# A Strassen form of the first MLP product in the last four tiles of a transformer block, and a plan that keeps GpSimd and VectorE apart

## The chip, the cores and the metric

One core of one Trainium2 chip runs the whole block. The metric is the device time of one launch in microseconds. Before the change the median of three runs was 514.28 us (513.51 to 523.58).

## What is computed

A pre-norm transformer block in float32 on x of 2048 tokens by D = 512: h = x + A(LN(x)), out = h + MLP(LN(h)).

- A: qkv = LN(x) wqkv (512 x 1536); 32 heads of 16; each token attends to 8 keys, itself and every second token back (offsets 0, 2, ..., 14), masked below 0; softmax; then the product with wo (512 x 512).
- MLP: relu(LN(h) w1 + b1) squared, times w2, plus b2, with F = 1792.

Every matmul operand is split into a high part (float32r, a cast on ScalarE) and a low part (the operand minus its high part); a product is three passes, high x high, high x low and low x high.

## The kernel before, in words

The 2048 tokens are 16 tiles of 128 rows; four tiles make a group u (`R = 4`, `NU = 4`). The hidden axis is 14 blocks of 128 (`FB`), called f. For a group, `mlp1(f)` multiplies a block of w1 (stationary, four K-blocks of 128) by the transposed normalised rows of the group (moving, 512 columns, kept in `big` as four K-blocks): 12 matmuls of 512 columns. ScalarE then applies relu with the bias, squares, and casts to the high part `rh`; GpSimd (or VectorE in the last group) makes the low part `rl`. `mlp2(f)` multiplies each tile's 128 columns of `rh` and `rl` (stationary) by the block of w2 (moving, 512 columns) and adds into four PSUM banks `acc`: 12 matmuls of 512 columns again. It runs two blocks behind `mlp1` (`LAGW = 2`). Before the first group come the first products (qkv) and attention. Attention is done in items, one for a group of tiles and a quarter of the heads: VectorE multiplies and reduces 2048-element rows, GpSimd adds up the weighted values, the result goes through DRAM to be transposed (`turned`), then through the product with wo (`wo_product`, line 457 for all three-pass products), the second norm and a second transposition. `split_h` writes the high and low parts of the next group into `big` once the current group's `mlp1` is through with it. Sums of the first three groups are parked in DRAM (`park`, `park_h`) and brought together with h and b2 by `unpark` during the last group, two sums for each of 12 tiles.

PSUM has eight banks: six slots `ps` (four of them `acc` during an MLP), `qp` and `le`.

The order is not written out by hand. Each step is a task with the engines that may run it, an estimated time on each, the keys it reads and writes, and a due time: for TensorE's tasks their place in TensorE's sequence, for others the earliest due time behind them less durations, or a `by` that the caller gave, moved by a small random draw (`NOISE`, `SEED`). `schedule` then simulates the engines and puts, at each step, the task with the earliest start (then the earliest due time) on its engine; buffers of each tag are counted, and some are kept free for the most urgent task (`KEEP`, `SPARE`). Attention items are due at `need[u] - ITEM * (G - g) - BEFORE[u]`. The program is issued in the order of the simulated start times; every engine works its own queue in that order, and all loads and stores are issued from SP. The waits between engines follow from what the instructions read and write, in the order of issue. The last lines of the function finish the group tile by tile, the last tile in two halves of 256 columns (line 955).

## Time and profile before

| | before |
|---|---|
| median of the runs | 514.28 us |
| the profiled execution | 514.67 us |
| its span, first to last instruction | 512.9 us |
| TensorE busy | 501.9 us, 2300 matmuls |
| VectorE, ScalarE, GpSimd busy | 333.6, 292.0, 323.0 us |
| DMA | 127.7 MB, mean 249 GB/s |

The span is 1.8 us shorter than the execution's time; the rest lies around it. PE is TensorE's matmuls, PEld its weight loads, DVE VectorE, ACT ScalarE, POOL GpSimd. A line such as L327 or L332 is that of a helper (`lo`, `tt`), so groups are told apart by the names of their tiles.

### The profile page before, as it was taken

What the parts mean: (1) busy time and instruction counts of PE and PEld (TensorE: products, weight loads), DVE (VectorE), ACT (ScalarE), POOL (GpSimd) and SP (SyncE); (2) the same over time, 40 slices, a digit from 0 to 9 for tenths busy, and PEclk for the clock granted to TensorE, in tenths of its full rate; (3) what the DMA queues carried; (4) which work ended last, traced back from release to release, by engine and by line L of the source; (5) the groups of instructions that cost most, each with busy time, mean ns of one, the idle gap of its engine ahead of it and who ended that gap; (6) DMA issues with size and microseconds to landing.
All of it is one profiled execution on the core that took longest, in us unless ns stands there. A gap on an engine that the chain in (4) does not pass through costs nothing.

```text
span 512.9 us, 6775 instructions
## 1 busy us (share of the span) xinstructions
PE 501.9 (98%) x2300; PEld 419.2 (82%) x2300; DVE 333.6 (65%) x314; ACT 292.0 (57%) x552; POOL 323.0 (63%) x273
## 2 busy tenths in 40 slices
PE   8999999999998999999999999999999999999997
PEld 8998888888886888868888877888888887888885
DVE  6259898996979996988799979596022103446003
ACT  4538877759364654379843436974367645433341
POOL 6421659768697799899994789589755424223220
PEclk9999999999999999999999999999999999999999
DMA  7699698999979999768976486865462731999422
GB/s 243 179 277 297 148 301 274 348 356 402 335 290 334 326 363 353 224 224 300 324 258 220 168 289 237 272 217 184 129 203 86 251 116 41 305 358 408 160 81 82
DMA packets 82834, 127.73 MB, mean 249 GB/s; under 512 B 7280, under 2 KB 49776, under 8 KB 82800
## 3 DMA queue, kind: packets, MB, share of 16 engines
q1 hardware_dynamic: 82656, 127.17, 73.3%
q8 instruction: 18, 0.29, 0.2%
q14 instruction: 16, 0.13, 0.1%
q10 hardware_dynamic: 144, 0.13, 0.1%
HBM read 89.96 MB, written 37.36 MB: 248 GB/s over the span
## 4 chain that ended last, share of the span: by engine, by line
PE 72%; DMA 8%; ACT 6%; POOL 5%; DVE 4%; issue 3%; SPq 1%; POOLq 0%; ACTq 0%; DVEq 0%
PE mm L457 41%; PE acc L735 20%; PE wo L457 7%; POOL pr L621 3%; DMA k<-qkv_d 3%; DVE pr L572 2%; PE tr L401 2%; DMA back<-o_d 2%; PE tr L803 1%; DMA qkv_d<-y 1%; DMA xt<-in_A_x_dram 1%; DMA o_d<-o 1%; POOL rl L327 1%; ACT r L722 1%; ACT big_h L322 1%
## 5 line engine op out<-in xcount | busy, mean ns | idle before, releaser
L621 POOL TENSOR_TENSOR pr<-pr 128x1024 f32<-128x1024 f32 (+1 forms) x64 | 118.8, 1883 | 11.7 <-DVE pr L603 8.4
L327 POOL TENSOR_TENSOR rl<-r,rh 128x512 fp32r<-128x512 f32 x53 | 68.6, 1297 | 86.4 <-ACT rh L322 86.2
L735 PE MATMUL acc<-w2s,rh 128*128 128x512 f32 x444 | 110.7, 389 | 0.0
L722 ACT ACTIVATE r<-mm,b_sb 128x512 f32<-128x512 f32 x56 | 38.3, 687 | 120.8 <-PE mm L457 113.8
L735 PEld LDWEIGHTS acc<-w2s,rh 128*128 128x128 f32 x444 | 83.3, 188 | 17.3
L572 DVE TENSOR_TENSOR pr<-qp,k 128x2048 f32<-128x2048 f32 x32 | 72.7, 2275 | 18.2 <-POOL o L621 12.7
L577 DVE TENSOR_REDUCE le<-pr 128x128 f32<-128x2048 f32 x32 | 73.3, 2290 | 0.9
L603 DVE TENSOR_TENSOR pr<-le,v 128x2048 f32<-128x2048 f32 x32 | 72.1, 2279 | 1.7 <-POOL o L621 1.1
L735 PE MATMUL acc<-w2s,rl 128*128 128x512 f32 x222 | 60.4, 390 | 0.0
L457 PE MATMUL mm<-big_h,xl 128*128 128x512 f32 (+1 forms) x208 | 51.1, 376 | 0.0
L457 PE MATMUL mm<-big_h,xh 128*128 128x512 f32 (+1 forms) x208 | 50.5, 375 | 0.1
L457 PE MATMUL mm<-big_l,xh 128*128 128x512 f32 (+1 forms) x208 | 50.6, 375 | 0.0
L735 PEld LDWEIGHTS acc<-w2s,rl 128*128 128x128 f32 x222 | 41.7, 188 | 9.0 <-DVE rl L327 0.4
L457 PEld LDWEIGHTS mm<-big_h,xh 128*128 128x128 f32 x208 | 38.0, 188 | 6.6 <-ACT big_h L322 0.5
L457 PEld LDWEIGHTS mm<-big_l,xh 128*128 128x128 f32 x208 | 37.9, 188 | 5.3
L457 PEld LDWEIGHTS mm<-big_h,xl 128*128 128x128 f32 x208 | 37.8, 188 | 5.2
L428 DVE STREAM_TRANSPOSE turned<-back 128x512 f32<-128x512 f32 x26 | 17.8, 696 | 36.6 <-DMA back<-o_d 24.1
L322 ACT CAST rh<-r 128x512 fp32r<-128x512 f32 x56 | 34.6, 622 | 3.0 <-ACT r L724 0.4
L724 ACT ACTIVATE r<-r 128x512 f32<-128x512 f32 x56 | 35.2, 632 | 1.3
L457 PE MATMUL mm<-big_h 128*128 128x512 f32 x128 | 34.5, 391 | 0.3 <-ACT r L722 0.3
L457 PE MATMUL mm<-big_h,big_l 128*128 128x512 f32 x128 | 34.2, 389 | 0.0
L457 PE MATMUL mm<-big_l,big_h 128*128 128x512 f32 x128 | 34.2, 389 | 0.0
(104 smaller groups left out, 791.2 us busy)
## 6 DMA issues: line engine op xcount, KB each, us to landing
w2s<-w_d SPq DMA_DIRECT2D x56, 512.0 KB, 5.0
k<-qkv_d SPq DMA_DIRECT2D x16, 704.0 KB, 6.1
v<-qkv_d SPq DMA_DIRECT2D x16, 704.0 KB, 6.2
qkv_d<-y SPq DMA_DIRECT2D x18, 512.0 KB, 3.6
raw<-in_B_w_dram SPq DMA_DIRECT2D x28, 256.0 KB, 6.7
w_d<-w2s SPq DMA_DIRECT2D x14, 512.0 KB, 6.6
xt<-in_A_x_dram SPq DMA_DIRECT2D x16, 256.0 KB, 5.7
q<-qkv_d SPq DMA_DIRECT2D x16, 256.0 KB, 4.3
```

Source lines behind the costliest of these rows:

```text
L322: act(n, lambda: nc.scalar.copy(dst(), src()), r=r, w=w, **k)
L327: lambda e: engines[e].tensor_tensor(out=dst(), in0=src(), in1=h(), op=ALU.subtract), r=r, w=w, **k)
L401: nc.tensor.transpose(tr.get()[:, n, :], s(), ident)
L428: vec(D, lambda: nc.vector.transpose(dst.get(), src.get()[:, part]), r=[src], w=[dst, *w])
L457: nc.tensor.matmul(ps(), l(), rr(), start=start and i == 0, stop=stop and i == len(terms) - 1)
L572: vec(2048, lambda pr=pr, i0=i0: nc.vector.tensor_tensor(out=pr.get(), in0=qp.get()[:, i0:i0 + IQ].unsqueeze(2).to_broadcast([P, IQ, W, GC ...
L577: vec(2048, lambda pr=pr, i0=i0: nc.vector.tensor_reduce(out=lg()[:, i0:i0 + IQ].rearrange("p i w h -> p (i w h)"), in_=pr.get().rearrange ...
L603: vec(2048, lambda p2=p2, i0=i0: nc.vector.tensor_tensor(out=p2.get(), in1=window(vs.get(), i0, [DH, GH], [1, DH]), op=ALU.mult, in0=ex()[ ...
L621: nc.gpsimd.tensor_tensor(out=dst, in0=a, in1=b_, op=ALU.add)
L722: act(D, lambda: nc.scalar.activation(r.get(), ps.get(), AF.Relu, bias=b1_sb[:, f:f + 1]), 0.08, r=[ps, "b1"], w=[r], keep=2)
L724: act(D, lambda: nc.scalar.activation(r.get(), r.get(), AF.Square), w=[r])
L735: nc.tensor.matmul(acc[j].get(), l.get()[:, j * P:(j + 1) * P], w2s.get()[:, wn], start=lead and n < len(js), stop=end and n >= len(terms) ...
```

## The change

In the last group the fourteen blocks f are taken in seven pairs (`WIN`). A pair's first product, a 256 x 512 by 512 x 512 product, is computed by the Winograd form of Strassen's scheme: both operands are cut into 2 x 2 blocks of 256 x 256, and seven products of sums stand for eight of blocks. A block product is 6 matmuls of 256 columns (two K-blocks, three passes), accumulated in half a PSUM bank. The sums of w1's blocks are made for each pair from raw weights that are loaded again (`win_weights`), one operand of each sum lying in PSUM, and their high and low parts go where wo's were. The sums of the rows are made once, on GpSimd or VectorE (`win_rows`), into two of the three `pr` buffers. The seven products are combined by seven sums on VectorE and one copy on ScalarE (`win_pair`), then follow relu, square and the split as before. The two sums of a parked tile move from VectorE to GpSimd. The plan no longer lets GpSimd and a VectorE task that is marked `port` (two operands in SBUF) overlap in its simulation, and hands a GpSimd task to VectorE when that ends sooner. The random draws come from one seed for each 40 us, and several constants of the plan are others.

```diff
-ITEM = 18.0
-BEFORE = 8, 4, 12, 8
+ITEM = 16.0
+BEFORE = 8, 16, 4, 16
 X_BY_DRAM = (14, 15)
-W2_EACH = 6.0
+W2_EACH = 4.5
 LO = ("POOL",)
 LAGW = 2
-NOISE, SEED = 0.3, 448
-LEAD = 10.0
+NOISE, SEEDS = 0.3, (
...
-AHEAD = 7.0
+AHEAD = 8.0
 WAIT = {"DVE": 1.2, "ACT": 0.6, "POOL": 1.6, "SP": 0.8}
-KEEP = 5
+KEEP = 4
 BUSY = 1.1
-SPARE = 1
+RENT = 1.6
+SPARE = 2
...
+        t.port = {"POOL"} | ({"DVE"} if port else set())
...
-                    s = max(free[eng], ready_at[t])
+                    f = max(free[eng], port) if eng in t.port else free[eng]
+                    s = max(f, ready_at[t])
...
+            if "DVE" in t.port and eng == "POOL" and "DVE" in t.eng:
+
+                v = max(s, free["DVE"])
+                if v + RENT * t.eng["DVE"] < s + t.eng["POOL"]:
+                    eng, s = "DVE", v
+            if eng in t.port:
+                port = end
...
-    def lo(n, dst, src, h, r, w, engs=("POOL", "DVE"), **k):
-        cost = {"POOL": po(n), "DVE": dv(n) if engs == ("DVE",) else dv(n) + 0.4}
+    def lo(n, dst, src, h, r, w, engs=("POOL", "DVE"), port=True, **k):
+        cost = {"POOL": po(n), "DVE": dv(n)}
         plan.add({e: cost[e] for e in engs},
                  lambda e: engines[e].tensor_tensor(out=dst(), in0=src(), in1=h(),
-                                                    op=ALU.subtract), r=r, w=w, **k)
+                                                    op=ALU.subtract), r=r, w=w, port=port, **k)
...
+        if WIN and t // R == NU - 1:
+            hts[i] = ht
+            if i >= RI:
+                to_split.append(lambda: win_rows(hts[i - RI], hts[i], i - RI))
...
+    TT = [buf("pr", (P, 4, D), F32R, "tt") for _ in range(2)]
+    def add_any(n, out_, a, b, op, **k):
+        plan.add({"POOL": po(n), "DVE": dv(n)},
+                 lambda e: engines[e].tensor_tensor(out=out_(), in0=a(), in1=b(), op=op),
+                 port=True, **k)
+    def win_rows(a, c, i):
+        t = buf("pair", (P, 4, 2 * P), name="t")
+        top, low = slice(0, 2), slice(2, 4)
+        tv = lambda n: t.get()[:, n].rearrange("p (k r b) -> p k b r", k=2, b=KB)
+        for n, x, y, r in (
+                (0, lambda: by_row(c)[:, top], lambda: by_row(a)[:, top], [a, c]),
+                (1, lambda: by_row(c)[:, low], lambda: tv(0), [c, (t, 0)]),
+                (2, lambda: by_row(c)[:, low], lambda: by_row(c)[:, top], [c]),
+                (3, lambda: tv(1), lambda: by_row(a)[:, low], [a, (t, 1)])):
+            add_any(256, lambda n=n: tv(n), x, y, ALU.subtract, r=r, w=[(t, n)])
+        def sums(part):
+            return TT[part].get().rearrange("p j (k s m) -> p (j k) s m", k=2, s=2)[:, :, i]
+        src = lambda: t.get().rearrange("p n (k m) -> p (n k) m", k=2)
+        ts = [(t, n) for n in range(4)]
+        hi(1024, lambda: sums(0), src, r=ts, w=[(TT[0], i)])
+        lo(1024, lambda: sums(1), src, lambda: sums(0), r=ts + [(TT[0], i)], w=[(TT[1], i)])
+    def win_b(part, n, kk):
+        if n < 3:
+            return big[part][:, (kk, 2 + kk, 2 + kk)[n], 2 * P * (n == 2):2 * P * (1 + (n == 2))]
+        return TT[part].get()[:, n - 3, 2 * P * kk:2 * P * (kk + 1)]
+    def win_b_keys(part, n):
+        if n < 3:
+            return B(part, ((0, 1), (2, 3), (2, 3))[n], (2, 3) if n == 2 else (0, 1))
+        return [(TT[part], 0), (TT[part], 1)]
+    def win_w(part, p, n):
+        if n < 3:
+            return w1_of(part, 2 * p + n // 2)[:, (0, 2, 2)[n]:(0, 2, 2)[n] + 2]
+        return wos[part][:, p % 2 * 2 + (n - 3) // 2].rearrange(
+            "p (n k c) -> p n k c", n=2, k=2)[:, (n - 3) % 2]
+    def win_w_keys(part, p, n):
+        if n < 3:
+            return w1_keys(part, 2 * p + n // 2)
+        return [("wo", part, p % 2 * 2 + (n - 3) // 2)]
+    def win_weights(p):
+        raw = buf("kv", (P, 4, 2 * P), name="raw1")
+        st = buf("le", (P, 2, 2 * P), name="st")
+        s34 = buf("o", (P, 2, 2 * P), name="s34")
+        A = lambda n: lambda: raw.get()[:, n]
+        S = lambda t, n: lambda: t.get()[:, n]
+        for j in range(2):
+            load(512, 512, lambda q, j=j: q.dma_start(
+                raw.get()[:, 2 * j:2 * j + 2].rearrange("p n (k c) -> p (n k) c", k=2),
+                w1_v[2 * p + j]), w=[(raw, 2 * j), (raw, 2 * j + 1)], ahead=2 * AHEAD)
+        act(256, lambda: nc.scalar.copy(S(st, 0)(), A(2)()), r=[(raw, 2)], w=[(st, 0)])
+        tt("DVE", 256, S(s34, 0), A(0), S(st, 0), ALU.subtract, r=[(raw, 0), (st, 0)],
+           w=[(s34, 0)])
+        tt("DVE", 256, S(st, 0), S(st, 0), A(3), ALU.add, r=[(raw, 3)], w=[(st, 0)])
+        tt("DVE", 256, S(st, 1), S(st, 0), A(0), ALU.subtract, r=[(raw, 0), (st, 0)], w=[(st, 1)])
+        tt("DVE", 256, S(s34, 1), A(1), S(st, 1), ALU.subtract, r=[(raw, 1), (st, 1)],
+           w=[(s34, 1)])
+        for j, t in enumerate((st, s34)):
+            keys = [[("wo", part, p % 2 * 2 + j)] for part in range(2)]
+            view = lambda part, j=j: wos[part][:, p % 2 * 2 + j]
+            src = lambda t=t: t.get().rearrange("p n c -> p (n c)")
+            r = [(t, 0), (t, 1)]
+            hi(D, lambda view=view: view(0), src, r=r, w=keys[0])
+            lo(D, lambda view=view: view(1), src, lambda view=view: view(0), r=r + keys[0],
+               w=keys[1], engs=("POOL", "DVE") if j else ("DVE",), port=j > 0)
+    def win_pair(p, after):
+        X_, Y, Z = (buf(tag, (P, 2, 2 * P), name="mm") for tag in ("ps", "ps", "qp"))
+        u = buf("o", (P, 2, 2 * P), name="u")
+        m1 = buf("q", (P, 2, 2 * P), name="m1")
+        rows = [[row(n, "A", dt=F32R) for n in ("rh", "rl")] for _ in range(2)]
+        r0, r1 = (row("r", "A", (P, 2, 2 * P)) for _ in range(2))
+        def product(bank, half, a, j):
+            def go(e):
+                out_ = bank.get()[:, half]
+                terms = [(0, 0), (1, 0), (0, 1)]
+                for m, (pa, pb) in enumerate(terms):
+                    for kk in range(2):
+                        nc.tensor.matmul(out_, win_w(pa, p, a)[:, kk], win_b(pb, j, kk),
+                                         start=m + kk == 0, stop=m + kk == len(terms))
+            keys = [k for part in range(2) for k in win_w_keys(part, p, a) + win_b_keys(part, j)]
+            plan.add({"PE": 6 * 0.1201}, go, r=keys + after,
+                     w=[(bank, half)] + ([(X_, 1), (Y, 0), (Y, 1)] if a == 0 else []))
+        def dve(out_, x, y, op, r, w):
+            tt("DVE", 2 * P, out_, x, y, op, r=r, w=w)
+        h = lambda t, n: lambda: t.get()[:, n]
+        product(X_, 0, 0, 0)
+        act(256, lambda: nc.scalar.copy(h(m1, 0)(), h(X_, 0)()), r=[(X_, 0)], w=[(m1, 0)])
+        product(X_, 1, 4, 4)
+        dve(h(u, 0), h(X_, 1), h(m1, 0), ALU.add, [(X_, 1), (m1, 0)], [(u, 0)])
+        product(Y, 0, 5, 5)
+        dve(h(u, 1), h(Y, 0), h(u, 0), ALU.add, [(u, 0), (Y, 0)], [(u, 1)])
+        product(Y, 1, 3, 3)
+        dve(h(r0, 1), h(Y, 1), h(u, 0), ALU.add, [(u, 0), (Y, 1)], [(r0, 1)])
+        dve(h(r1, 1), h(Y, 1), h(u, 1), ALU.add, [(u, 1), (Y, 1)], [(r1, 1)])
+        product(Z, 0, 2, 6)
+        dve(h(r1, 0), h(u, 1), h(Z, 0), ALU.subtract, [(u, 1), (Z, 0)], [(r1, 0)])
+        product(X_, 0, 1, 1)
+        dve(h(r0, 0), h(X_, 0), h(m1, 0), ALU.add, [(X_, 0), (m1, 0)], [(r0, 0)])
+        product(X_, 1, 6, 2)
+        dve(h(r0, 1), h(X_, 1), h(r0, 1), ALU.add, [(X_, 1)], [(r0, 1)])
+        for f, r, (rh, rl) in ((2 * p + 1, r1, rows[1]), (2 * p, r0, rows[0])):
+            flat = lambda r=r: r.get().rearrange("p n c -> p (n c)")
+            both = [(r, 0), (r, 1)]
+            act(D, lambda f=f, flat=flat: nc.scalar.activation(
+                flat(), flat(), AF.Relu, bias=b1_sb[:, f:f + 1]), 0.08, r=["b1"], w=both)
+            act(D, lambda flat=flat: nc.scalar.activation(flat(), flat(), AF.Square), w=both)
+            hi(D, rh.get, flat, r=both, w=[rh])
+            lo(D, rl.get, flat, rh.get, r=both + [rh], w=[rl])
+        return rows
...
-        tt("DVE", D, m.get, m.get, b2_row[0].get, ALU.add, r=[b2_row[0]], w=[m], by=due + 5)
-        tt("DVE", D, m.get, m.get, h.get, ALU.add, r=[h], w=[m, ("turn", t % 3)], by=due + 5)
+        tt("POOL", D, m.get, m.get, b2_row[0].get, ALU.add, r=[b2_row[0]], w=[m], by=due + 5)
+        tt("POOL", D, m.get, m.get, h.get, ALU.add, r=[h], w=[m, ("turn", t % 3)], by=due + 5)
...
+        pairs = [2 * p for p in WIN] if last else ()
+        f = done = 0
+        while f < FB:
+            fs = (f, f + 1) if f in pairs else (f,)
             if u == 0 and f + FA < FB:
                 w1_job(FA + f)
-            w2s[f] = get_w2(f)
-            hid[f] = mlp1(f, ("DVE",) if last and f >= FB - LAGW else engs)
-            if f >= 2:
-                g = f - 2
+            for g in fs:
+                w2s[g] = get_w2(g)
+            if f in pairs:
+                win_weights(f // 2)
+                hid[f], hid[f + 1] = win_pair(f // 2, [("second", u)] if f > 2 else [])
+            else:
+                hid[f] = mlp1(f, ("DVE",) if last and f >= FB - LAGW else engs)
+            f = fs[-1] + 1
+            for g in range(done, f - LAGW):
                 if last and g == FB - 1 - LAGW:
                     mlp2(g, hid[g], w2s[g], acc, range(R - 1), g == 0, False, True)
                     mlp2(g, hid[g], w2s[g], acc, [R - 1], g == 0, True, False)
                 else:
-                    mlp2(g, hid[g], w2s[g], acc, range(R), g == 0, False, True)
-            if not last and f == TO_MLP:
+                    mlp2(g, hid[g], w2s[g], acc, range(R), g == 0, False, True,
+                         [("second", u)] if g == 0 else [])
+                done = g + 1
```

## Rows read from the trace of the kernel before

**Rows 1.** The page, busy time of each engine: us, share, instructions

```profile
PE 501.9 (98%) x2300; PEld 419.2 (82%) x2300; DVE 333.6 (65%) x314; ACT 292.0 (57%) x552; POOL 323.0 (63%) x273
```

**Rows 2.** Stretches of the span: us, busy us of each engine (count), clock, DMA

```profile
core 0: us, PE busy (x) PEld busy (x) DVE busy (x) ACT busy (x) POOL busy (x), PEclk, DMA share, GB/s
0.00:156.00 156.00, 154.12 (x770) 134.78 (x771) 122.33 (x122) 100.90 (x220) 99.87 (x106) 1.00 0.88 288
156.00:168.00 12.00, 9.96 (x50) 8.02 (x49) 11.93 (x11) 7.15 (x14) 9.18 (x7) 1.00 0.97 338
168.00:430.00 262.00, 258.64 (x1131) 211.12 (x1130) 172.87 (x148) 156.21 (x276) 197.38 (x150) 1.00 0.68 232
430.00:500.00 70.00, 70.00 (x310) 57.97 (x309) 21.46 (x27) 25.75 (x41) 16.59 (x13) 1.00 0.67 240
500.00:513.00 13.00, 9.14 (x46) 7.34 (x44) 4.99 (x8) 2.01 (x4) 0.00 (x0) 1.00 0.22 81
```

**Rows 3.** TensorE's waits: us in total, times, longest us

```profile
PE mm L457 <- DVE big_l L327: 2.0, 1, 2.0
...
PE wo L457 <- ACT oh L322: 1.9, 2, 1.2
...
PE tr L803 <- POOL ident masks.py:199: 1.3, 1, 1.3
```

**Rows 4.** The chain of waits in order of time: start us, us, what

```profile
122.12 1.93 PE tr L401 x16
...
480.74 1.81 PE mm L457 x8
...
507.71 1.44 PE half L955 x12
```

**Rows 5.** VectorE's groups: form xcount | busy us, mean ns | idle before

```profile
L327 DVE TENSOR_TENSOR big_l<-turned,big_h 128x512 fp32r<-128x512 f32 x4 | 7.5, 1901 | 17.6 <-ACT big_h L322 17.6
...
L327 DVE TENSOR_TENSOR rl<-r,rh 128x512 fp32r<-128x512 f32 x3 | 2.1, 692 | 31.9 <-ACT rh L322 31.9
```

**Rows 6.** ScalarE's groups of the MLP

```profile
L722 ACT ACTIVATE r<-mm,b_sb 128x512 f32<-128x512 f32 x56 | 38.3, 687 | 120.8 <-PE mm L457 113.8 <-POOL big_l L327 4.6 <-POOL pr L621 2.3
...
L724 ACT ACTIVATE r<-r 128x512 f32<-128x512 f32 x56 | 35.2, 632 | 1.3
...
L322 ACT CAST rh<-r 128x512 fp32r<-128x512 f32 x56 | 34.6, 622 | 3.0 <-ACT r L724 0.4
```

**Rows 7.** GpSimd's groups, one plain and one strided low part

```profile
L327 POOL TENSOR_TENSOR rl<-r,rh 128x512 fp32r<-128x512 f32 x53 | 68.6, 1297 | 86.4 <-ACT rh L322 86.2
...
L327 POOL TENSOR_TENSOR ol<-turned,oh 128x512 fp32r<-128x512 f32 x12 | 18.7, 1574 | 6.4 <-ACT oh L322 6.2
```

**Rows 8.** All waits, those of the parked sums

```profile
DVE m L332 <- DMA m<-m_d: 7.7, 8, 1.8
...
DVE m L332 <- DMA h<-h_d: 4.0, 4, 2.0
```

**Rows 9.** DMA issues: count, KB each, median us to landing

```profile
raw<-in_B_w_dram SPq DMA_DIRECT2D x28, 256.0 KB, 6.7
```

**Rows 10.** Timeline, change to the last group: start us, us, engine

```profile
408.08 0.71 DVE L428 STREAM_TRANSPOSE turned<-back 128x512 f32<-128x512 f32 x1 [2.09 <-DMA back<-t_d]
...
424.30 2.95 ACT L322 CAST big_h<-turned 128x512 fp32r<-128x512 f32 x3 [1.56 <-PE mm L457]
...
428.76 1.19 PE L457 MATMUL mm<-big_h,w1a_h 128*128 128x512 f32 x4 [0.87 <-ACT big_h L322]
```

**Rows 11.** The timeline, GpSimd and VectorE in the last group

```profile
450.34 1.29 POOL L327 TENSOR_TENSOR rl<-r,rh 128x512 fp32r<-128x512 f32 x1 [6.56 <-ACT rh L322]
...
450.62 1.56 DVE L332 TENSOR_TENSOR m<-m,b 128x512 f32<-128x512 f32 x1 [1.73 <-DMA m<-m_d]
```

**Rows 12.** The timeline, the last matmul and the sum that waits for it

```profile
508.86 0.28 PE L955 MATMUL half<-w2s,rh 128*128 128x256 f32 x1
...
509.18 0.42 DVE L332 TENSOR_TENSOR h<-half,h 128x256 f32<-128x256 f32 x1 [0.29 <-PE half L955]
```

More of the change, by code (lines that the diff above doesn't have):

```diff
@@ L34 @@
 WARM = 46
-ITEM = 18.0
-BEFORE = 8, 4, 12, 8
+ITEM = 16.0
+BEFORE = 8, 16, 4, 16
 X_BY_DRAM = (14, 15)
-W2_EACH = 6.0
+W2_EACH = 4.5
 LO = ("POOL",)
 LAGW = 2
-NOISE, SEED = 0.3, 448
-LEAD = 10.0
+NOISE, SEEDS = 0.3, (
+    487, 765, 735, 246, 644, 701, 83, 442, 213, 893, 112, 220, 567, 914)
+WIN = (0, 1, 2, 3, 4, 5, 6)
+LEAD = 6.0
 BY_PE = (0,)
@@ L84, in add @@
     def add(self, eng, fn, r=(), w=(), by=None, dma=None, ahead=None, first=None,
-            keep=None, lead=0.0):
+            keep=None, lead=0.0, port=False):
         t = Task()
@@ L129, in deadlines @@
     def deadlines(self):
-        draw = random.Random(SEED)
+        draws = [random.Random(n) for n in SEEDS]
         for t in reversed(self.tasks):
@@ L134, in deadlines @@
             t.alap = t.pe if t.pe is not None else d if t.by is None else min(d, t.by)
+            draw = draws[max(0, min(int(t.alap // 40), len(draws) - 1))]
             t.due = t.alap + draw.uniform(-NOISE, NOISE)
@@ L150, in schedule @@
         queue = {tag: sorted((t for t in self.tasks if any(b.tag == tag for b in t.new)),
-                             key=lambda t: t.due) for tag in (*ROWS, "pair")}
+                             key=lambda t: t.due) for tag in (*ROWS, "pair", "pr")}
         while ready:
@@ L175, in schedule @@
                         continue
-                    key = (s if s > free[eng] + 0.02 else free[eng],
+                    key = (s if s > f + 0.02 else f,
                            t.due - 1e3 if t.pe is not None and t.early else t.due, t.n)
@@ L179, in schedule @@
                         pick = key, t, s
-                if pick and (best is None or pick[2] < best[2]):
+                if pick and (best is None or (pick[2], pick[1].due) < (best[2], best[1].due)):
                     best = eng, pick[1], pick[2]
@@ L187, in schedule @@
                             held.setdefault(b.tag, {})[b] = t
-                raise RuntimeError([(o.n, round(o.start), round(o.due)) for o in order
-                                    if o.on == "PE"][::40], [(t.n, [b.tag for b in t.new]) for t in ready][:12],
+                raise RuntimeError([(t.n, t.fn.__code__.co_firstlineno, round(t.due), [b.tag for b in t.new]) for t in ready],
                                    {k: [(t.n, users[b]) for b, t in v.items()]
@@ L289, in block_kernel @@
     w1a = (w1a_h, w1a_l)
-    le = psum.tile([P, 2, R * W * GH], F32, name="le")
     bufs = {**ROWS, "pair": 4, "unit": 1, "kv": 3, "q": 1, "pr": 3, "o": 2, "ps": 6, "qp": 1,
-            "st": 2, "mv": 4, "rs": 4, "sv": 6, "mx": 2, "sm": 2}
+            "le": 1, "st": 2, "mv": 4, "rs": 4, "sv": 6, "mx": 2, "sm": 2}
     pools = dict.fromkeys(("st", "mv", "rs", "sv", "mx", "sm"), small)
-    pools.update(ps=psum, qp=psum, unit=wpool, pair=wpool)
+    pools.update(ps=psum, qp=psum, le=psum, unit=wpool, pair=wpool)
     plan = Plan(bufs)
@@ L579, in item @@
                 in_=pr.get().rearrange("p i w (h d) -> p (i w h) d", d=DH), axis=X, op=ALU.add),
-                r=[pr], w=[("lg", i0)], by=due + 5 * n + 1)
+                r=[pr], w=[(LE, i0)], by=due + 5 * n + 1)
         if u < 2:
@@ L605, in item @@
                 in0=ex()[:, i0:i0 + IQ].unsqueeze(4).to_broadcast([P, IQ, W, GH, DH])),
-                r=["ex", vs], w=[p2], by=due + 9 + i0)
+                r=[exs, vs], w=[p2], by=due + 9 + i0)
             w = W // 2
@@ L688, in parts @@
             lo(D, lambda: view(1), src, lambda: view(0), r=[ht] + keys[0],
-               w=keys[1], engs=("DVE",) if pe else ("POOL", "DVE"))
+               w=keys[1], engs=("DVE",) if pe else ("POOL", "DVE"), port=not pe)
         to_split.append(parts)
+        if WIN and t // R == NU - 1:
+            hts[i] = ht
+            if i >= RI:
+                to_split.append(lambda: win_rows(hts[i - RI], hts[i], i - RI))
     w2_d = [dram.tile([P, 2, D], F32, name="w2_d") for _ in range(FB)]
@@ L727, in mlp1 @@
         return rh, rl
-    def mlp2(f, hid, w2s, acc, js, first, last, split_):
+    TT = [buf("pr", (P, 4, D), F32R, "tt") for _ in range(2)]
[19 more added lines that the diff above has]
+        lo(1024, lambda: sums(1), src, lambda: sums(0), r=ts + [(TT[0], i)], w=[(TT[1], i)])
@@ L730, in mlp2 @@
+    def mlp2(f, hid, w2s, acc, js, first, last, split_, more=[]):
         rh, rl = hid
@@ L737, in go @@
                                      stop=end and n >= len(terms) - len(js))
-            plan.add({"PE": len(terms) * 0.23}, go, r=r, w=[acc[j] for j in js])
+            plan.add({"PE": len(terms) * 0.23}, go, r=r, w=[acc[j] for j in js] + more)
         one = [(rh, 0, j) for j in js] + [(rh, 1, j) for j in js]
@@ L905, in to_mlp @@
                              out=h[i].get(), in0=h[i].get(), in1=b2_row[0].get(), op=ALU.add),
-                         r=[b2_row[0]], w=[h[i]], by=plan.pe + 20)
+                         r=[b2_row[0]], w=[h[i]], by=plan.pe + 20, port=True)
     to_mlp(0, need[0])
@@ L927, in block_kernel @@
                 else:
-                    mlp2(g, hid[g], w2s[g], acc, range(R), g == 0, False, True)
-            if not last and f == TO_MLP:
+                    mlp2(g, hid[g], w2s[g], acc, range(R), g == 0, False, True,
+                         [("second", u)] if g == 0 else [])
+                done = g + 1
+            if not last and TO_MLP in fs:
                 to_mlp(u + 1, need[u + 1])
```

23 lines of the change are left out of this document (12 added, 11 removed).

## The prediction

> **What bounds the kernel now.** I began with the busy totals of the page. TensorE is busy for 501.9 of 512.9 us, VectorE, GpSimd and ScalarE for 65, 63 and 57% [rows 1]: the reader is to see that only work or waits of TensorE can move the end by much. Then the windows, which say where the 11 us without TensorE work lie: 1.9 before 156 us (1.3 of it ahead of the first transpose), 2.0 between 156 and 168, 3.4 from 168 to 430, none in the 70 us of the last group's MLP (430 to 500), and 3.9 behind 500, where the last sums go out [rows 2, 3]. The list of TensorE's waits names who ended these gaps: VectorE's low part of `big` once for 2.0 us, ScalarE's high part of `o` twice for 1.9 together [rows 3]. The granted clock is 1.00 (2.4 GHz) throughout [rows 2]. Last, the chain of waits gives TensorE's pace: eight 512-column matmuls in 1.81 us, 0.2263 each, and twelve 256-column ones in 1.44 us, 0.120 each [rows 4]. So in the stretch that the change rewrites, the end is set by TensorE's own column count and nothing else.
>
> **The products.** Per pair of F-blocks the two first products are 24 matmuls of 512 columns: 24 x 0.2263 = 5.43 us. Strassen's form has 7 products of 6 matmuls of 256 columns: 42 x 0.120 = 5.04 us. An eighth of the columns goes, and the shorter matmul gives part of it back, because its cost is 0.120 and not half of 0.2263. The gain is 0.39 us a pair, 2.7 us over seven pairs. Bounds: at exactly half a 512-column matmul (0.113) it is 4.8 us; at the 0.1206 of the sixteen transposes [rows 4] it is 2.6. I take 0.120, since those twelve are the same operation at the same width, each with its own weight load as here. By the Trainium skill, "TensorE: Matmul & The Clock Gate", section on the back-to-back gap, a warm matmul takes N/2.4 + 2.5 ns, 109 ns at 256 columns and 216 at 512; the gain would then be 4.2 us, but both rows are slower than the rule, and I keep the rows.
>
> **What the pairs ask of the other engines.** One pair with the two second products beside it lasts 5.04 + 24 x 0.2263 = 10.5 us. VectorE gets 11 operations on 256 columns with one operand in PSUM and one 512-column low part: 11 x 0.42 + 0.69 = 5.3 us [rows 5, 12]. ScalarE gets two 256-column copies (at most a 512-column cast each, 0.62), two such casts and twice relu, square and cast: 1.24 + 1.24 + 3.88 = 6.4 us [rows 6]. GpSimd gets at most three low parts, 3.9 us, and 24 parked sums in all, 24 x 1.30 = 31 us over seven pairs, 4.5 a pair [rows 7]: 8.4 of 10.5 us, the fullest of the three, but not full. I cost all this at nothing; TensorE's 10.5 us cover it. If the cover went, GpSimd would be the first to run over, and the low parts `rl` would be late for the second product.
>
> **The waits that it adds.** (a) The parked sums wait for their loads, and stand now ahead of low parts in GpSimd's queue. On VectorE there were 12 such waits, 11.7 us together, the longest 2.0 [rows 8], with nothing of weight behind them. A pair's low parts are due when the next pair's products are done, 10.5 us after its own; the chain to them is two sums, two times relu, square and cast, and one low part: 0.85 + 3.88 + 1.30 = 6.0 us. The 4.5 us left over hold the longest wait and a sum ahead of it (2.0 + 1.3): nothing. For the last pair only the 5.43 us of second products stand behind it; its first chain starts two products early, so that the second ends about 4.3 us after the last product. Nothing again. (b) Fourteen more loads of 256 KB of raw weights go through SP's queue ahead of later loads, and to the DMA engines: 3.7 MB in 70 us are 52 GB/s on the 240 of that stretch, which brings the share from 0.67 to about 0.82 [rows 2]. Such loads took 6.7 us to land [rows 9] and are asked for 16 us ahead. The parked loads slide: a tile's two sums take 2.6 us on GpSimd for 1.4, and as every third tile waits for the one before, its loads and its store on SP come up to 4 x 1.2 = 5 us later; only the end waits for them, and they are due from 76 us before it at 5 us a tile. Nothing. (c) The first pair needs the four row sums of `t` with their high and low parts. The last transposed row was there at 408.8 us, and `big` was free to be overwritten from 424.3 [rows 10]. All eight sums and both 1024-column low parts on GpSimd, at the rate of its strided 512-column low part (1.57) [rows 7], are 8 x 0.8 + 2 x 3.1 = 12.6 us, and half of it can be done before the last row comes. Covered, and the first product needs only two of the four rows of `big`.
>
> **Keeping GpSimd and VectorE apart.** The trace shows what is avoided: a VectorE sum of two SBUF operands that began 0.28 us into a GpSimd operation took 1.56 us where one alone takes 0.69, and GpSimd's kept its 1.29 [rows 5, 11]. In the last 70 us this costs TensorE nothing. Before 430 us it matters where such low parts stand between TensorE and its input: the split of `big` at the change of groups, where VectorE's strided low parts took 1.9 us on average [rows 5] and TensorE waited. What it can give is bounded by TensorE's idle time there, 7.3 us less the 1.3 at the start: 6.0 us [rows 2, 3]. As the whole plan is drawn again (new due times for attention, other draws, other reserves), I bound the loss by the same: as much idle time again, 6 us. Between -6 and +6 I take a gain of 1.0: about the one gap of 0.87 us at the change to the last group [rows 10], which the first pair's smaller need should close, and nothing net elsewhere.
>
> **The sum** stands against the profiled execution: 512.9 us of span and 1.8 around it, 514.67. Less 2.7 and 1.0 it is 511.0; the median of the runs lies 0.4 under the profiled one, so 510.6, which I call 510.5.
>
> **The rivals.**
> *Forecast* (0.60): TensorE stays bound, 2.7 us go from the products and waits give back up to 3 us or cost up to 1: 507.5 to 512.5.
> *The plan recovers most of the waits* (0.12): with the collisions gone the attention chain and the splits come in time, and of the 6.0 us four to six go: 514.3 - 2.7 - 5 = about 506.5, range 505 to 507.5. For it: VectorE ended the largest wait. Against: that one stood behind attention work, not behind a collision.
> *The new plan loses what Strassen gains* (0.18): attention items that fall due earlier for the second and fourth group (by up to 10 us) and later for the first and third (by up to 16) collide with the splits elsewhere, and 2 to 6 us of waits come back: 514.3 - 2.7 + 4 = 515.5, range 512.5 to 518. For it: VectorE is 78% busy up to 156 us and full in the next 12 [rows 2], so what comes sooner for one group comes later for another. This is also the case in which keeping the engines apart is only planned: no wait is added that would enforce it.
> *Two halves of one bank* (0.10), the case on the other side: a pair has only three PSUM banks for seven products, and three times a product writes one half while ScalarE or VectorE has to read the other. If the product is held until the reader is through, TensorE loses each time the end of the last matmul (0.28, less the 0.12 it would have taken), the reader's 0.42 and two hand-offs of about 0.04 [rows 12]: 0.66 us. That is 2.0 us a pair, 13.9 over seven, less 2.7: 525.5, and some 528 where the next weight load is late as well. It decides from 0.62 us a product on: (10.3 + 2.7) / 21. Against it: the plan puts each product right behind the last one and each reader behind its product's end, so the reader comes second in the order and it is the reader that waits, one product longer; three other products lie between it and the next writer of that bank. No row of before has a bank shared in this way. The Trainium skill, "PSUM — Partial Sum Buffer", section on bank collisions, speaks for it: two engines in one bank and the same 32 partitions collide whichever bytes they touch, and it asks for a guard by bank.
>
> **The numbers.** What this measurement can tell from no change is about 2%, 10.3 us: below 504.0 or above 524.6. Below 504.0 needs every wait gone and the products at their better bound: 0.03. Above is the bank case, less the part in which only some of the 21 products are held: 0.09. Within: 0.88. The range leaves out that case and the ends of the others: 505.5 to 516.
>
> **What would show it.** Right: the twelve-matmul pace again, 42 short matmuls in 5.0 us, no TensorE wait inside a pair; the last group's stretch some 2.7 us shorter; parked sums on GpSimd at 1.3 us, and VectorE's two-operand work back at 0.69. Wrong: TensorE waits on sums or copies of `mm` inside the pairs (the bank case), on `rl` behind parked sums (GpSimd over), on `tt` at the first pair, or more than 6 us of idle time between 10 and 430 us.

## The result, and the profile after

The changed kernel takes 519.4 us (median of 6 runs, 518.32 to 520.14) against 514.44 for the kernel before beside it: ratio 1.0100, 95% interval 1.0079 to 1.0120. I had forecast 510.5, range 505.5 to 516. It is slower, not faster, though by less than 2%. The time of some kernels below includes disturbed runs, which the ratios leave out, so comparisons go by the ratios.

The busy totals of the page after, which answer to [rows 1]:

```profile
span 518.3 us, 7193 instructions
PE 502.3 (97%) x2426; PEld 423.8 (82%) x2426; DVE 369.3 (71%) x406; ACT 302.1 (58%) x582; POOL 334.0 (64%) x282
```

TensorE is busy for 0.4 us more than before, although it has fewer columns to multiply, and the span is 5.4 us longer. The windows after, in the stretches of [rows 2]:

```profile
core 0: us, PE busy (x) PEld busy (x) DVE busy (x) ACT busy (x) POOL busy (x), PEclk, DMA share, GB/s
0.00:156.00 156.00, 154.34 (x775) 135.48 (x775) 127.38 (x127) 100.74 (x220) 94.93 (x98) 1.00 0.90 302
156.00:168.00 12.00, 9.40 (x42) 7.61 (x42) 11.77 (x15) 6.31 (x12) 11.50 (x12) 0.90 0.92 302
168.00:430.00 262.00, 254.75 (x1109) 207.03 (x1108) 180.95 (x171) 153.92 (x278) 184.01 (x141) 1.00 0.68 230
430.00:500.00 70.00, 69.16 (x427) 61.28 (x426) 42.06 (x82) 37.38 (x67) 43.53 (x33) 1.00 0.81 269
```

Two things stand out beside [rows 2]. Between 168 and 430 us TensorE is idle for 7.3 us where it was 3.4. And in the 12 us before that the mean granted clock is 0.90 where it was 1.00. The waits of TensorE after, for [rows 3]:

```profile
PE mm L469 <- ACT big_h L334: 4.2, 3, 1.8
PE mm L469 <- ACT r L742: 2.1, 2, 1.1
PE acc L880 <- ACT rh L334: 1.7, 2, 1.4
PE tr L948 <- POOL ident masks.py:199: 1.3, 1, 1.3
PE tr L413 <- ACT hn L374: 1.1, 1, 1.1
PE wo L469 <- ACT oh L334: 0.8, 1, 0.8
PE mm L840 <- ACT m L850: 0.7, 2, 0.4
```

VectorE's `big_l` (2.0 us before) is gone from the list. ScalarE's results, `big_h`, `r`, `rh` and `hn`, have come in its place, for 9.1 us where they were 1.4. Between 10 and 430 us TensorE is idle for 10.2 us, 5.9 before: over the 6 that the prediction gave as a sign of being wrong.

**Where the time went.** Up to the first product of the last group both kernels issue the same 1942 matmuls, in places in another order, and behind it there are 178 second products and 12 short ones in both. So the start of the n-th matmul can be compared, after less before:

| time in before, us | 107 | 125 | 145 | 166 | 187 | 207 | 229 | 250 | 271 | 313 | 354 | 420 | first product |
|---|---|---|---|---|---|---|---|---|---|---|---|---|---|
| after later by, us | -1.7 | -1.7 | -0.7 | 0.4 | 1.4 | 2.9 | 3.9 | 4.8 | 6.8 | 5.4 | 7.0 | 7.2 | 6.2 |

The first product starts at 434.93 us, 428.76 before [rows 10]: +6.17. From there to the last matmul's end it is 79.69 us for 80.38: -0.69. The tail is 3.68 for 3.74. The sum, +5.4, is the difference of the spans. The loss is complete before a Strassen product is issued. Of the 7.2 us at 420 us the first product gives 1.0 back, since the wait ahead of it (1.26 us from start to start before) is gone.

What moved there is attention. VectorE's operations on `pr`, the 2048-column ones of attention, by stretch, after and then before (busy us and count of these alone, clock, DMA):

```profile
160.00:200.00 40.00, 25.25 (x12) 0.96 0.77 256
200.00:230.00 30.00, 22.60 (x11) 1.00 0.83 281
```

```profile
160.00:200.00 40.00, 32.11 (x15) 1.00 0.98 348
200.00:230.00 30.00, 17.87 (x8) 1.00 0.73 258
```

Three of them slide from 160 to 200 us into the next 30; at 230 us the count is the same again, 64 for 63. What TensorE asks of attention moved more. The product with wo of the second group is its 1023rd matmul here and was its 1047th, 24 matmuls or 5.4 us of work sooner in its order, while the rows for it come back from memory at nearly the same time (after, then before):

```profile
218.08 0.71 DVE L440 STREAM_TRANSPOSE turned<-back 128x512 f32<-128x512 f32 x1 [0.61 <-DMA back<-o_d]
```

```profile
218.83 0.71 DVE L428 STREAM_TRANSPOSE turned<-back 128x512 f32<-128x512 f32 x1 [0.21 <-DMA back<-o_d]
```

So up to there TensorE has less work to fill the time with. That this is what opens the gaps of 199 to 219 us is my reading of the order; no run changes it alone.

One of the new waits in full, in the timeline after (start us, us, engine, line, idle before and releaser):

```profile
159.30 1.29 POOL L339 TENSOR_TENSOR w2s<-raw,w2s 128x512 fp32r<-128x512 f32 x1
160.68 0.22 POOL L366 TENSOR_SCALAR rs<-mv 128x1 f32<-128x1 f32 x1
161.95 0.81 ACT L374 ACTIVATE hn<-h,rs 128x512 f32<-128x512 f32 x1 [2.85 <-POOL rs L370]
162.82 0.75 PE L413 MATMUL tr<-ident,hn 128*128 128x128 f32 x4 [1.08 <-ACT hn L374]
165.09 1.32 PE L469 MATMUL mm<-big_h,w1a_h 128*128 128x512 f32 x3 [1.51 <-ACT big_h L334]
```

A low part of W2 that TensorE does not wait for stands on GpSimd ahead of the three tiny operations that scale a row of the norm. ScalarE waits 2.85 us for them, TensorE 1.08 for ScalarE, and the next MLP's first product 1.5 more for the casts behind that. Then the clock:

```profile
161.00:165.10 4.10, 1.50 (x11) 1.09 (x9) 3.87 (x7) 3.15 (x7) 4.00 (x4) 1.00 0.97 265
165.10:168.60 3.50, 3.50 (x9) 2.81 (x10) 3.32 (x4) 0.90 (x2) 3.50 (x5) 0.56 1.04 407
```

After 4.1 us in which TensorE worked for 1.5, the granted clock is 0.56 over 3.5 us, mostly the lower level (1.2 GHz). Seven of the matmuls there start 0.427 us apart instead of 0.227; with the edges that is 1.7 us. The Trainium skill, "TensorE: Matmul & The Clock Gate", section "Wait — 56ns, not 53.3ns?", gives 426.7 ns for 512 columns at that level; the trace agrees.

**Inside the pairs** the forecast pace holds, two 256-column matmuls in 0.24 us, but four waits are new. One of them:

```profile
455.20 1.09 PE L880 MATMUL acc<-w2s,rl 128*128 128x512 f32 x4
455.73 0.56 ACT L334 CAST wo_h<-st 128x512 fp32r<-128x512 f32 x1
456.19 0.37 ACT L850 COPY m<-mm 128x256 f32<-128x256 f32 x1
456.62 0.50 PE L840 MATMUL mm<-tt,wo_h 128*128 128x256 f32 x2 [0.32 <-ACT m L850]
```

The plan has put four second products (`acc`) between the first product and the second. So the copy of the first (L850) stands ahead of the second product in the program, and TensorE waits until the copy is through, though the copy reads the other half: both halves are one tile, which fills one PSUM bank. It is so at 436.6, 455.9 and 485.3 us, with 0.75, 0.72 and 0.42 us from start to start for 0.227, and the second matmul behind each is another 0.10 late: 1.5 us. In three other pairs the `acc` matmuls cover the copy. A fourth gap (0.41 at 445.1, 0.4 us lost) is of another kind. The plan has put the second pair's fifth product right behind its first, and the weight load ahead of it waits for VectorE:

```profile
445.04 0.41 DVE L344 TENSOR_TENSOR r<-u,mm 128x256 f32<-128x256 f32 x1
445.50 0.30 PEld L840 LDWEIGHTS mm<-tt,w1a_h 128*128 128x128 f32 x2 [0.33 <-DVE r L344]
```

This sum reads the first pair's fifth product, and there is only one buffer (`qp`) for the fifth products of all pairs.

The parked sums, now on GpSimd, and the strided low parts of `big` left to VectorE:

```profile
L344 POOL TENSOR_TENSOR m<-m,h 128x512 f32<-128x512 f32 x12 | 16.1, 1346 | 0.4
L344 POOL TENSOR_TENSOR m<-m,b 128x512 f32<-128x512 f32 x12 | 15.7, 1314 | 8.6 <-DMA m<-m_d 8.5
L339 DVE TENSOR_TENSOR big_l<-turned,big_h 128x512 fp32r<-128x512 f32 x6 | 6.7, 1160 | 0.9 <-PE mm L469 0.9
```

### The profile page after: what moved, and what is told of

Read it like the earlier page. It is cut to its first block, busy times and chain, and to the rows that moved or that the text cites. A ratio compares the mean times of both kernels' runs of the same rounds, so it can differ in the third digit from the quotient of the medians.

```text
span 518.3 us, 7193 instructions
## 1 busy us (share of the span) xinstructions
PE 502.3 (97%) x2426; PEld 423.8 (82%) x2426; DVE 369.3 (71%) x406; ACT 302.1 (58%) x582; POOL 334.0 (64%) x282
## 4 chain that ended last, share of the span: by engine, by line
PE 40%; POOL 11%; issue 6%; ACT 5%; DMA 5%; DVE 5%; SPq 1%; POOLq 0%; ACTq 0%; DVEq 0%
PE acc L880 17%; PE mm L469 11%; PE mm L840 6%; PE wo L469 4%; POOL pr L637 4%; DMA raw<-in_B_w_dram 2%; DVE pr L587 2%; ACT big_h L334 2%; DMA back<-o_d 2%; DMA back<-t_d 1%; POOL rl L339 1%; POOL o L637 1%; POOL ol L339 1%; POOL w2s L339 1%; DVE le L592 1%
## 5 line engine op out<-in xcount | busy, mean ns | idle before, releaser
L637 POOL TENSOR_TENSOR pr<-pr 128x1024 f32<-128x1024 f32 (+1 forms) x64 | 117.4, 1848 | 7.3 <-DVE pr L619 6.8
L339 POOL TENSOR_TENSOR rl<-r,rh 128x512 fp32r<-128x512 f32 x48 | 63.2, 1317 | 60.8 <-ACT rh L334 50.4
L742 ACT ACTIVATE r<-mm,b_sb 128x512 f32<-128x512 f32 x42 | 28.8, 686 | 72.0 <-PE mm L469 68.3
L469 PE MATMUL mm<-big_h,xl 128*128 128x512 f32 (+1 forms) x208 | 49.7, 375 | 0.0
L469 PE MATMUL mm<-big_l,xh 128*128 128x512 f32 (+1 forms) x208 | 49.0, 374 | 0.0
L546 ACT COPY y<-mm 128x512 f32<-128x512 f32 x36 | 20.7, 587 | 14.9 <-PE mm L469 9.6
L469 PE MATMUL mm<-big_h 128*128 128x512 f32 x96 | 25.9, 394 | 2.1 <-ACT r L742 2.1
L744 ACT ACTIVATE r<-r 128x512 f32<-128x512 f32 x42 | 26.6, 634 | 1.0
L396 POOL TENSOR_TENSOR sv<-sv,mhalf 128x1 f32<-128x1 f32 x24 | 13.1, 549 | 21.7 <-ACT sv L394 21.6
```

Source lines behind the costliest of these rows:

```text
L339: lambda e: engines[e].tensor_tensor(out=dst(), in0=src(), in1=h(), op=ALU.subtract), r=r, w=w, port=port, **k)
L469: nc.tensor.matmul(ps(), l(), rr(), start=start and i == 0, stop=stop and i == len(terms) - 1)
L546: act(D, lambda: nc.scalar.copy(y.get()[:, :, j, :], ps.get().rearrange("p (j c) -> p j c", c=GC)), r=[ps], w=[(y, j)], by=plan.pe + 3)
L637: nc.gpsimd.tensor_tensor(out=dst, in0=a, in1=b_, op=ALU.add)
L742: act(D, lambda: nc.scalar.activation(r.get(), ps.get(), AF.Relu, bias=b1_sb[:, f:f + 1]), 0.08, r=[ps, "b1"], w=[r], keep=2)
L744: act(D, lambda: nc.scalar.activation(r.get(), r.get(), AF.Square), w=[r])
```

## Experiments

**1. The new plan without Strassen.** `WIN = ()`; the order is the same up to some 379 us.

```diff
-WIN = (0, 1, 2, 3, 4, 5, 6)
+WIN = ()
```

> The changed kernel with no pair in the Strassen form (all fourteen first products of the last group as before); plan, draws and parked sums as in the changed kernel, and the simulated order is the same up to about 379 us. Theory A, the loss lies in the newly drawn plan of the first 430 us (TensorE reached the last group at 434.9 us instead of 428.8): 520 to 522, slower than before by 1.1 to 1.5%, and slower than the changed kernel by the 0.7 to 2.7 us that Strassen gives. Theory B, what the Strassen form asks for (buffers, sums, loads) disturbs the stretch before: about 514.4, as before.

520.34 us, ratio 1.0111 (1.0092 to 1.0130), as expected: the loss is there without one Strassen product. The last group's first product starts 5.4 us later than before. The same gaps stand at 161, 163, 199, 213, 219 and 242 us, the half clock between 166 and 169.

**2. Strassen on the old plan.** The settings, prices, order of ties and draws of the kernel before; only tasks of the last group get draws of their own. The order is that of before up to some 386 us; the parked sums stay on VectorE.

```diff
-        t.port = {"POOL"} | ({"DVE"} if port else set())
+        t.port = set()
...
-            draw = draws[max(0, min(int(t.alap // 40), len(draws) - 1))]
-            t.due = t.alap + draw.uniform(-NOISE, NOISE)
+            late = t.n >= self.late or t.win
+            t.due = t.alap + (own if late else draw).uniform(-NOISE, NOISE)
```

> The kernel before with the Strassen form alone: old constants, old draws (tasks that are new or belong to the last group draw from another stream, so that the simulated order is the same as before up to 386 us), no port rule, parked sums on VectorE. Theory A: 0.7 to 2.7 us faster than before, 511.7 to 513.7 beside 514.4; TensorE reaches the last group at 428 to 429 us. Theory B: 4 to 6 us slower than before, 518 to 520.

Ratio 0.9980 (0.9960 to 1.0000): the loss is gone, and Strassen is worth 1 us, not 2.7. From the first product to the last matmul it is 80.35 us, as before (80.38): waits inside the pairs take back what the products save.

**3. The kernel before with another draw.** Only the seed is changed.

```diff
-NOISE, SEED = 0.3, 448
+NOISE, SEED = 0.3, 4
```

> The kernel before with another seed for the small draws on the due times (4 for 448), nothing else. Theory A in its stricter form, any new draw costs, because the old one is a lucky one: 3 us more by the plan's own simulated end (510.0 beside 507.0), so 516 to 519. Rival, the draws are harmless and it is the new constants or the port rule that cost: 513.5 to 515.5.

516.03 us, ratio 1.0029 (1.0015 to 1.0043), the lower edge of what I expected. A draw alone moves the time by 0.3%, with its waits in other places (2.40 us at 43.7, 1.91 at 74.7; the 2.44 at 163.8 shrunk to 0.84).

**4. The same as 2, with the parked sums on GpSimd.**

```diff
-        tt("DVE", D, m.get, m.get, b2_row[0].get, ALU.add, r=[b2_row[0]], w=[m], by=due + 5)
+        tt("POOL", D, m.get, m.get, b2_row[0].get, ALU.add, r=[b2_row[0]], w=[m], by=due + 5)
```

> The Strassen form on the old plan, and the two sums of each parked tile on GpSimd instead of VectorE. The prediction's cost of nothing for this move: the same as the form on the old plan within 0.5 us. Rival, low parts wait in GpSimd's queue behind parked sums: 1 to 4 us slower than it, with TensorE's waits on `rl` in the last group.

Ratio 0.9974 (0.9952 to 0.9997), 0.9980 without: the move costs nothing that these intervals (0.2%) can show.

**5. Products in twos.** Two products that share a bank become one task, so that nothing can be placed between them.

```diff
-        product(X_, 0, 0, 0)
+        product(X_, (0, 0, 0), (1, 4, 4))
         act(256, lambda: nc.scalar.copy(h(m1, 0)(), h(X_, 0)()), r=[(X_, 0)], w=[(m1, 0)])
-        product(X_, 1, 4, 4)
```

> Strassen on the old plan with the parked sums on GpSimd, but two products that share a PSUM bank are one item of the plan (products 1+2, 4+5, 7+8 in the order of the code), so that nothing can come between them. Theory (the waits inside the pairs come from a reader of one half of a bank that is placed between the two products, so that the second product must wait for it): the gaps at 436.8 (0.41), 447.6 (0.99) and 460.6 us (0.33) go, 0.2 + 0.8 + 0.1 = 1.1 us; time 512.8, ratio to before 0.995. Rival (the sums themselves are late, the bank has nothing to do with it): gaps of the same size stay inside the pairs and the time is that of the version it is made from, 513.9, ratio 0.997.

Ratio 0.9942 (0.9921 to 0.9962). The only wait of a Strassen product that is left, against two in kernel 4:

```profile
PE mm L855 <- DVE big_l L343: 0.5, 1, 0.5
```

```profile
PE mm L854 <- ACT m L864: 0.6, 1, 0.6
PE mm L854 <- DVE big_l L343: 0.5, 1, 0.5
```

From the first product to the last matmul it is 78.36 us, 80.09 in kernel 4 and 80.38 before. The four gaps of kernel 4 inside its pairs (0.41, 0.99, 0.30, 0.33 from start to start), reckoned as above, are 1.6 of these 1.7 us; all are gone. The expectation gives all of them to a reader of half a bank that is placed between two products. By the weight loads' waits the 0.41 at 436.8 us is not of that kind: it is the wait for the one `qp` buffer again (`r<-u,mm`), and goes because the fifth product now comes later in the order.

**6. The changed kernel, one exchange on GpSimd.** The W2 low part of the timeline above goes behind the norm's scale.

```diff
+MOVES = ((904, 959),)
...
+    for n, behind in MOVES:
+        t, seq = plan.tasks[n], seqs[plan.tasks[n].on]
+        seq.remove(t)
+        seq.insert(seq.index(plan.tasks[behind]) + 1, t)
```

> The changed kernel with one exchange in its planned order: on GpSimd the three small operations for the norm's row scale (rs) come ahead of the low part of W2 that stood in front of them; all else as planned. Theory (the new plan loses by its order at single places): the norm comes 1 us sooner, the gap of TensorE at 161.5 us (1.36) falls below 0.4, the next at 163.3 (1.80) stays or shrinks; if the half clock of 165 to 168 us goes with it, 1.75 us more are won: 516.6 with it, 518.4 without it, against 519.4. Rival (what is saved here is given back at the next stall): 519.4, with 1.80 at 163.3 grown to about 2.8.

519.78 us, ratio 1.0091 (1.0062 to 1.0120): nothing won. The gap at 161 shrank from 1.36 to 0.45 and the half clock at 165 went, but `r` was then awaited at 198 us for 2.9 us, and the half clock came there. ScalarE has `r` behind the copy `qp`, which waits for attention:

```profile
198.02 2.29 DVE L588 TENSOR_TENSOR pr<-qp,k 128x2048 f32<-128x2048 f32 x1 [5.56 <-POOL o L638]
200.34 0.59 ACT L581 COPY qp<-q 128x512 f32<-128x512 f32 x1 [6.05 <-DVE pr L588]
```

That is not all of it: in this trace the last group's first product starts 1.2 us sooner than in the changed kernel's, and the 1.2 us are lost behind it, where the wait for the copy `m` at 456 us is 1.36 us instead of 0.32.

**7. Four more exchanges.** On ScalarE a copy `qp`, a weight's cast and a norm behind ready work of the MLP, on GpSimd that weight's low part.

```diff
-MOVES = ((904, 959),)
+MOVES = ((904, 959), (586, 1056), (1023, 1070), (1024, 1071), (1148, 1098))
```

> The same, and four more exchanges at the gaps of 199, 213 and 242 us: on ScalarE the copy qp and the cast of a weight, both waiting for something else, and a norm come behind the relu and square that stand ready and that TensorE waits for; on GpSimd that weight's low part behind rl. Theory (heads of queues that wait hold up ready work; the loss is the sum of these places): gaps at 161.5, 199.4, 212.6 and 241.9 us fall by 1.1 + 1.2 + 1.5 + 1.1 = 4.9 us, and 1.75 if the half clock goes: 512.8 to 514.5. Rival (the waits move on to later places, since attention comes later): over 517.

521.17 us, ratio 1.0111 (1.0081 to 1.0141). The rival held. The gaps at 213, 219 and 242 us went, and one of 4.25 at 217 took their place; the wait and the timeline there:

```profile
PE wo L470 <- ACT oh L335: 3.9, 1, 3.9
```

```profile
219.15 0.71 DVE L441 STREAM_TRANSPOSE turned<-back 128x512 f32<-128x512 f32 x1 [1.57 <-DMA back<-o_d]
219.89 1.11 ACT L335 CAST oh<-turned 128x512 fp32r<-128x512 f32 x1 [3.89 <-DVE turned L441]
221.06 1.15 PE L470 MATMUL wo<-wo_h,oh 128*128 128x512 f32 x2 [3.86 <-ACT oh L335]
```

TensorE has caught up with the second group's attention, whose result comes back from memory (`o_d`) at 219 us (218 in the changed kernel), whatever was moved on ScalarE. The small gaps were not the bound there; attention was.

**8. Kernel 5 and one exchange on VectorE.** The product of attention that stood ahead of four low parts of `big` at the first MLP goes behind them.

```diff
+MOVES = ((461, 971),)
```

> The version with products in twos on the old plan, and one exchange: on VectorE the product pr of attention (2.29 us) that stood ahead of four low parts of big at the first MLP comes behind them. Theory: the largest gap of the kernel before (2.44 us at 163.8, 2.42 here) shrinks to under 0.5, nothing is given back: 512.8 - 2.0 = 510.8, ratio 0.991 to 0.992. Rival (attention comes 2.3 us later and the gap comes back at 220 to 245 us, where the o rows are awaited): 512.8, with gaps of 2 us more in sum between 200 and 250 us.

509.0 us (508.38 to 510.32), ratio 0.9892 (0.9869 to 0.9915). It beats both kernels; 510.8 was expected. The 2.0 us of `big_l` [rows 3] are gone; about 1 came back at 218 us, where `oh` is now awaited longer:

```profile
PE wo L474 <- ACT oh L339: 2.4, 2, 1.7
PE tr L963 <- POOL ident masks.py:199: 1.3, 1, 1.3
PE mm L856 <- DVE big_l L344: 0.5, 1, 0.5
```

**9 and 10. One half of the new plan on kernel 5:** the rule with its prices and its order of ties, and the settings.

```diff
-        t.port = set()
+        t.port = {"POOL"} | ({"DVE"} if port else set())
...
-                if pick and (best is None or pick[2] < best[2]):
+                if pick and (best is None or (pick[2], pick[1].due) < (best[2], best[1].due)):
...
-        cost = {"POOL": po(n), "DVE": dv(n) if engs == ("DVE",) else dv(n) + 0.4}
+        cost = {"POOL": po(n), "DVE": dv(n)}
```

```diff
-ITEM = 18.0
-BEFORE = 8, 4, 12, 8
+ITEM = 16.0
+BEFORE = 8, 16, 4, 16
...
```

> The version with products in twos on the old settings and draws, and of the new plan only the rule that keeps GpSimd and VectorE's two-operand work apart (with its prices). The plan's own simulation of it ends at 518.9 us, where that of the version it is made from ends at 505.1 (measured 512.2), with waits of TensorE at 43, 164 and 257 us in it. Theory A (any new drawing of the plan loses, as the draws belong to the settings): half to all of the 13.8 us shows, 519 to 526. Theory B (the rule is not what costs; collisions avoided repay it): 511 to 514, and VectorE's two-operand work on 512 columns stays near 0.7 us.

> The same version with only the new settings (ITEM, BEFORE, W2_EACH, LEAD, AHEAD, KEEP, SPARE) on the old draws, without the rule. The plan's own simulation ends at 517.2. Theory A (any new drawing loses): 518 to 524, with gaps of TensorE about 165 and 258 us. Theory C (the loss of the changed kernel is in the rule alone): 511 to 514.

530.25 us, ratio 1.0284 (1.0250 to 1.0318), and 522.18, ratio 1.0143 (1.0116 to 1.0171), where kernel 5 has 0.9942. Each half alone, on draws that were not made for it, loses more than both with theirs. But here most of the loss stands in the plan's own simulation, which ends at 518.9 and 517.2 us, 505.1 for kernel 5. In 9 TensorE waits:

```profile
PE mm L473 <- ACT big_h L338: 7.0, 3, 3.9
PE mm L473 <- DVE h L348: 4.0, 1, 4.0
PE tr L417 <- ACT xn L406: 1.9, 3, 1.0
```

**11. The kernel before and the exchange of 8, no Strassen.** The diff is that of 8.

> The kernel before with the one exchange on VectorE (the product pr behind four low parts of big at the first MLP), no Strassen. Theory (the exchange is worth what it removes, less what attention gives back at 218 us): gap of 2.44 at 163.8 us under 0.5, the one at 219.7 grown by 1.0: 513.6, ratio 0.998. Then Strassen in twos is worth 3 us on this plan as on the other (509.0 against it is a ratio of 0.991 to 0.992). Rival (the exchange won all, and Strassen little): 511.5.

512.15 us, ratio 0.9950 (0.9931 to 0.9969). Against 8 (0.9892) Strassen in twos is worth 0.58%, 3.0 us, as between kernel 5 and before (0.58%). The exchange is worth 2.6 us in both places, where I had expected 1 here. Part of that may be the clock: all 13 runs of 8 and 11 show a mean granted clock of 0.999 or 1.000, most runs of before do not (below).

**12. The changed kernel with products in twos,** the diff of 5.

> The changed kernel with products in twos and nothing else; the plan is the same up to about 400 us. Theory (waits at the shared bank): the gaps inside the pairs (0.75, 0.41, 0.72, 0.42) go, 1.4 us less: 518.0, ratio 1.007. Rival (the plan about the pairs puts waits elsewhere; its own simulation ends 1.4 us later): 519.4 to 520.

516.89 us, ratio 1.0037 (1.0023 to 1.0051): 0.6% under the changed kernel, more than the 1.4 us expected. TensorE waits no more for ScalarE's `m`, and the gap at 445 us is gone as well. From the first product to the last matmul it is 78.76 us, 0.9 less than in the changed kernel, with a new wait of 0.7 for `rl` at 492 us. Another 1.2 us of the two traces' difference stands ahead of the first product, and I can't say why, since the planned order is the same up to about 400 us.

## Why the prediction was wrong, point by point

- **The plan drawn again: the step that failed.** I took a gain of 1.0 between -6 and +6. It lost 6.2 us before the first product, at the end of the bound: 4.2 us more of idle time and 1.7 of half clock. The mechanism was that of the third case, "The new plan loses what Strassen gains", to which I gave 0.18; its top, 518, was too low, since neither the bank's waits nor the clock was in it. I had taken the row of one visible wait (0.87 us at the change to the last group [rows 10]) as the likeliest size of a redrawing that touches every row. That gap did close, and gave the 1.0 us that I had put down for it: TensorE goes into the first product without a wait. What failed is "nothing net elsewhere": 7.2 us were lost ahead of it, and between 125 and 271 us alone some 8.5.
- **Which part of the plan.** Not settled. The rule alone and the settings alone both lose (9, 10), as does a mere new draw (3). But the plans of 9 and 10 end late in their own simulation, that of the changed kernel does not, so they need not lose by the same cause; and its 14 seeds and its handling of the buffers `le` and `pr` are in neither. What runs 6 and 7 show is the form of the loss: TensorE asks for the second group's attention sooner than it comes, and gaps taken away ahead of it come back in front of it.
- **The half clock** was not in my sum: the trace of before has none. It costs 1.7 us here and follows the two waits in a row. That trace was a lucky one. Of the 59 runs of before that stand behind the ratios of 1 to 12, 41 show a mean granted clock of 0.992 to 0.997 and take 515.3 us on average; the 18 with 0.998 to 1.000 take 513.9. All six of the changed kernel show 0.995 to 0.997. So in most of its runs before pays some 1.4 us too, and only part of the 1.7 sets the two kernels apart.
- **The products** were sized right: -2.7 forecast. In kernels 5 and 8 the stretch from the first product on is 2.0 us shorter than before, with 0.8 us of a wait in it (0.82 from start to start for 0.12, and 0.07 behind it), so -2.8. These 2.0 us and the 1.0 us of the wait ahead of the first product are the 3.0 us of 8 against 11. In the changed kernel 1.9 us of gaps inside the pairs and 0.3 at the first product leave -0.7.
- **Two halves of one bank** was a rival with 21 held products and 0.66 us each. Three were held in this way, at 0.3 to 0.6 us. My ground against it, that each product stands right behind the last, does not hold: in five pairs the plan has put second products of an earlier block between the first and the second, the second and the third, and the third and the fourth, and in a sixth between the first two. In the changed kernel it costs time only between the first and the second; in kernel 4 the 0.33 is between the third and the fourth. The Trainium skill, "PSUM — Partial Sum Buffer", section "PSUM bank collisions raise a hardware error", wants the guard by bank; here the program's order enforces one. What the chip does without it no run here shows, nor whether the order goes by the bank or by the tile that fills it.
- **What was costed at nothing** held. The parked sums on GpSimd took 1.31 and 1.35 us and delayed nothing that shows (4 against 2). The DMA share from 430 to 500 us is 0.81, forecast 0.82. TensorE's waits for `tt` and `rl` do not appear; the tail is the same.
- **Keeping the engines apart** is only planned, and works in part: six strided low parts on VectorE take 1.16 us on average, less than the 1.90 of [rows 5]. That is the rule's doing: with it they take 1.12 to 1.18 us (kernels 1, 9, 12), without it 1.90 to 1.97 (4, 5, 8, 10). TensorE gains nothing by it, since it waits for ScalarE there.

Open is why the new plan, whose own simulation ends at 507.1 us like the old one's 507.0, runs 12.3 us longer on the chip and the old one 7.4. In the other drawings it is 4.9 (10), 6.0 (3), 6.6 (5), 8.4 (12), 9.0 (2), 10.8 (1) and 11.4 us (9): the simulated end tells the chip's to within some 4 us either way. Its prices miss some durations in all of them; I have not tried to mend them.

## What to carry to other kernels

Where a change redraws a whole schedule, that is a term of its own, of several us and either sign, and it is measured only by replaying the old order under the new work (2) and the new order without it (1). A gap of the busiest engine is worth what it removes only if what comes next is early: look up who is awaited after it before counting it (7 against 8). One trace is one execution: look through the mean granted clocks of all runs before taking its stretches for the kernel's. Two results in one PSUM bank are best issued in one piece, readers behind both.

## What the runs showed of the hardware that I had not expected

- Half clock after a wait. Waits of TensorE of 2.0 us (kernel 5, at 163 us), 2.9 (6, at 198) and 3.9 (7, at 217) were followed by a granted clock of 0.52 to 0.64 over the next 3.5 to 4.3 us. The 2.0 us of before [rows 3] and 1.8 us in kernel 6 at 163.5 were not; the same 1.8 us in kernel 7 were (0.67 over 4.7 us). So at about 2 us it went both ways, in the same place of nearly the same program. Both kernels without the wait at 163.8 us (8, 11) show a mean clock of 0.999 or 1.000 in every run.
- GpSimd and VectorE hold each other up both ways. Before, VectorE's sum that began second took 1.56 us [rows 11]. After, GpSimd's took longer when it began second:

```profile
466.41 0.73 DVE L339 TENSOR_TENSOR rl<-r,rh 128x512 fp32r<-128x512 f32 x1
466.67 1.62 POOL L344 TENSOR_TENSOR m<-m,h 128x512 f32<-128x512 f32 x1
```

  That is 0.33 us over the 1.29 of one alone; VectorE's operation ended 0.47 us after GpSimd's began. The Trainium skill, "SBUF — State Buffer", section "SBUF: two separate sides", states that whichever starts first holds the shared port for its whole instruction; both rows agree in who loses.
